# A hand-written order for the first feed-forward stage, with its first-batch products in the rounds that end attention

## The chip, the cores and the metric

One core of a Trainium2 chip. The metric is the device time of one execution in microseconds; a time is the median of several executions. Engines: PE (TensorE, matrix products), PEld (its weight loads), DVE (VectorE), ACT (ScalarE), POOL (GpSimd), SP (the queue that issues the DMAs).

## The reference

Three stages on two batches (B = 2) of 448 tokens, 12 heads of 64:

```python
scores = scale * np.matmul(q, k.transpose(0, 1, 3, 2))      # causal mask, then softmax
attn_out = np.matmul(attn, v)                               # to x: (B, S, 768)

x_prev = x shifted by one token
xk = mu_k * x + (1.0 - mu_k) * x_prev
xr = mu_r * x + (1.0 - mu_r) * x_prev
k = np.maximum(xk @ w_k, 0.0)                               # 768 -> 1024
v = k * k @ w_v                                             # 1024 -> 768
r = 1.0 / (1.0 + np.exp(-(xr @ w_r)))                       # 768 -> 768
x2 = r * v

h = np.maximum(x2 @ w_in, 0.0)                              # 768 -> 1024
gate = sigmoid(conv over 3 tokens of h)
out = (h * gate) @ w_out                                    # 1024 -> 768
```

The weights come as 64-bit floats.

## The kernel before, in words

Every large product is made of three matmuls (mm3, L63): each operand is split in a high half, rounded to the fast format, and a low half, what the rounding left; high by high, high by low and low by high are summed in PSUM. The high half of a tile is made by split_h (L68), the low half by split_l (L76), a subtraction on DVE or POOL. On the profile's lines the three matmuls of every product are L64, L65 and L66, the high halves L70 (POOL) and L74 (ACT), the low halves L78.

Attention runs as a pipeline of 12 jobs, one for a batch and a pair of heads. One round of the pipeline touches five jobs at once (n, c, l, p, a: from the next job to the one three rounds ago). What each engine does in a round, and in which order, is a written list, ORDER (L426). In it kqT transposes q and k, sc makes the scores, red the row minima (DVE), exp the exponentials (ACT), norm the division (POOL), T the transposes of the probabilities (L290), C the copies of them out of PSUM (ACT, or DVE for banks 3 and 4), V the products with v (L307), out the copy to xT (ACT), and mixP, mixD, mixH, mixL the token mix xr of one job for the next stage, with mixP, mixH and mixL on POOL and mixD on DVE. The loop of rounds, i from -1 to 14, stands in a manual schedule, so this order is kept on PE, ACT, DVE and POOL. In the rounds 12 to 14 there is no next and no current job, and their entries are left out. In the first rounds small matmuls on the identity (keep_warm, L443) stand behind some entries.

The first feed-forward stage has weight columns wr0 to wr5 (128 columns of w_r each), then wk0 to wk7 (w_k), wv0 to wv5 (w_v), and the second wi0 to wi7 (w_in) and rows wo0 to wo7 (w_out). Each is loaded as raw 64-bit words (load, L111, tag "wraw", two buffers, issued by SP) and converted (convert, L126) in seven steps: Abs on ACT (L100), four integer steps on DVE (L102, L104, L106, L108), the high half on ACT (L74) and the low half on DVE (L78). The converted pair goes to one of three buffers (tag "whl"). A call of step does one of the seven, convert_next all that are left. In rounds 4 to 11 of attention the entries w call step; two weight columns are ready by the end of the loop, and a third and most of a fourth follow right behind (L466).

For each column the stage makes products with xr (768 inputs in six chunks) for both batches (token_mm, L359), pr0 to pr5; ACT copies them to sr, and mix makes one chunk of xk for both batches: scaling on ACT (L339), the sum on DVE (L343), the high half on ACT, the low half on POOL (L78). The products with w_k (pk), w_v (pv) and w_in (ph) follow in the same way. Outside the manual schedule a scheduler sets the order of the engines by its own estimate of the time: it may move a stage's instructions up between those of attention.

Of the kernel before, what the change touches and what calls it, by code (L numbers as in the profile page):

```python
# [13 lines left out]
AF = mybir.ActivationFunctionType  # L14
# [5 lines left out]
def kernel(  # L20
# [105 lines left out]
    def convert(raw, n, name, he, le, rows=False, own=()):  # L126
# [23 lines left out]
        fill=-1e9 / SCALE, base=0, pattern=[[-1, CP]], channel_multiplier=1,  # L150
# [37 lines left out]
    def big(tag, name):  # L188
        return (act if tag in early else act2).tile([P, 2, NT], F32R, tag=tag, name=name)
# [6 lines left out]
    xr = [big(f"Y{c}", f"xr{c}") for c in range(NC)]  # L196
# [10 lines left out]
    class Job:  # L207
# [59 lines left out]
        def exp(self, c, j):  # L267
            w, i = (c + 1) * CP, 2 * c + j
            self.p[j, c] = p = sp.tile([CP, w], F32, tag=f"p{c}{j}", name=f"p_{self.n}_{i}", bufs=2)
            nc.scalar.activation(  # L270
                p, self.s[c, j][:, :w], AF.Exp, bias=self.st[:, 0, i:i + 1], scale=-1.0,
                accum_out=self.st[:, 1, i:i + 1],
            )
# [51 lines left out]
            mix_l(1, xr[self.hp], self.b, self.hp)  # L325

        def w(self, _):
            if 4 <= self.i < 11:
                step()

    ms = {}

    def mix_p(kind, b, c):
        ms[kind, b, c] = m = mixp.tile([P, S], F32, tag="m", name=f"m{kind}_{b}_{c}")
        prev, a = xT[c][:, b, 0:S], kind * NC + c
        if kind:
            nc.gpsimd.tensor_scalar(m, prev, mu[:, 2 * NC + a:2 * NC + a + 1], 1.0, ALU.mult, ALU.mult)  # L337
        else:
            nc.scalar.activation(m, prev, AF.Copy, scale=mu[:, 2 * NC + a:2 * NC + a + 1])  # L339

    def mix_d(kind, b, c):
        m, a = ms[kind, b, c], kind * NC + c
        nc.vector.scalar_tensor_tensor(m, xT[c][:, b, 1:S + 1], mu[:, a:a + 1], m, ALU.mult, ALU.add)  # L343

    def mix_h(kind, dst, b, c):
        split_h("p" if kind else "s", dst[:, 0, TOK[b]], ms[kind, b, c])

    def mix_l(kind, dst, b, c):
        split_l("p", dst[:, 1, TOK[b]], ms[kind, b, c], dst[:, 0, TOK[b]])

    def mix(kind, dst, b, c):
        mix_p(kind, b, c)
        mix_d(kind, b, c)
        mix_h(kind, dst, b, c)
        mix_l(kind, dst, b, c)

    TOK = [slice(b * S, (b + 1) * S) for b in range(B)]

    def token_mm(name, w, x, late):  # L359

        n = len(x)
        out_ = [bank(f"{name}_{b}") for b in range(B)]
        for c, b in sorted(((c, b) for b in range(B) for c in range(n)), key=lambda k: (late and k[0] == n - 1, k[1])):
            t = TOK[b]
            wt, o = w[0], slice(c * P, c * P + P)
            mm3(out_[b], wt[:, 0, o], wt[:, 1, o], x[c][:, 0, t], x[c][:, 1, t], c == 0, c == n - 1)
        return out_

    ring = ["mm"]

    def bank(name):
        tag = ring[0]
        ring.append(ring.pop(0))
        return ps.tile([P, 512], F32, tag=tag, name=name, bufs={"sc": 4, "tr": TR, "po": PO}[tag])[:, :S]
# [32 lines left out]
    def step():  # L407

        if not running:
            running.append(steps_next())  # L410
        if next(running[0], running) is running:
            running.clear()

    def convert_next():
        step()
        while running:
            step()

    def take():

        while loaded and not loaded[0][0] and len(ready) <= AHEAD:
            convert_next()
        return ready.pop(0)
# [9 lines left out]
    ROUNDS_AGO = {"n": -1, "c": 0, "l": 1, "p": 2, "a": 3}  # L433
    order = [x.split(".") for x in ORDER.split()]
    jobs = []
    small_steps = small()
# [6 lines left out]
    def keep_warm(n):  # L443
        for _ in range(n):
            nc.tensor.matmul(warm[:, :P], ident, ident, start=True, stop=True)

    keep_warm(7)
    ET = mybir.EngineType
    with tc.manual_schedule(engines={ET.PE, ET.Activation, ET.DVE, ET.Pool}):
        for i in range(-1, B * NPAIR + 3):  # L450
            if 2 <= i + 2 < B * NPAIR:
                jobs.append(Job((i + 2) // NPAIR, (i + 2) % NPAIR))
                jobs[-1].load()
            if i in (0, 1, 2):
                next(small_steps, None)
            if i == 2:
                load_next()
            for who, what, *a in order:
                x = i - ROUNDS_AGO[who]
                if 0 <= x < B * NPAIR and (i >= 0 or who == "n"):  # L460
                    getattr(jobs[x], "T_" if what == "T" else what)(*(int(y) if y.isdigit() else y for y in a))

                    if i < 1 and what in ("kqT", "sc", "T"):
                        keep_warm(3)

    convert_next()  # L466
    for _ in range(5):
        step()
    actx.close()
    ring[:] = ["sc", "sc", "tr", "sc", "sc", "tr", "tr", "po"]  # L470
    act2 = ctx.enter_context(tc.tile_pool(name="act2", bufs=1, reuse_waits="tile"))
    xk = [big(f"X{c}", f"xk{c}") for c in range(NC)]
    sr = [act2.tile([P, NT], F32, tag=f"U{e}", name=f"sr{e}") for e in range(NE)]
    for e in range(NE):
        w = take()
        for b, pr in enumerate(token_mm(f"pr{e}", w, xr, e == 0)):
            nc.scalar.activation(sr[e][:, TOK[b]], pr, AF.Copy)
        for b in range(B):
            mix(0, xk[e], b, e)
    pinned[0] = False  # L480
    wo_t = act.tile([P, 7, 2, WT], F32R, tag="T", name="wo_t")
    wo_slots += [wo_t[:, i] for i in range(7)]
# [2 lines left out]
    for f in range(NF):  # L485
        w = take()
        k2.append(big(f"Y{f}", f"k2_{f}"))
        for b, pk in enumerate(token_mm(f"pk{f}", w, xk, f == 0)):
            t = TOK[b]
            a = mixp.tile([P, S], F32, tag="m", name=f"a{f}_{b}")  # L490
# [8 lines left out]
    for e in range(NE):  # L499
        w = take()  # L500
        x2.append(big(f"X{e}", f"x2_{e}"))
        tc.keep_in_program_order(nc.scalar.activation(sr[e], sr[e], AF.Sigmoid))
        for b, pv in enumerate(token_mm(f"pv{e}", w, k2, e == 0)):
            t = TOK[b]
            a = mixp.tile([P, S], F32, tag="m", name=f"xv{e}_{b}")
# [9 lines left out]
    for f in range(NF):  # L515
        w = take()
# [29 lines left out]
    for o0 in range(0, len(outs), 6):  # L546
# [46 lines left out]
```

## Time and profile before

| | us |
|---|---|
| median of 3 executions | 406.72 (406.42 to 408.78) |
| the profiled execution | 408.7 |
| its span in the trace | 406.9 |
| PE busy | 390.5 (96%) |
| DVE busy | 307.4 (76%) |
| ACT busy | 233.8 (57%) |
| POOL busy | 126.1 (31%) |

Attention takes the time to about 119, the products with w_r to 165, those with w_k to 225, w_v to 285, w_in to 344, w_out to the end. In the timelines a row gives the start and the length of one instruction or of several like ones, and in brackets how long the engine stood idle before it and what ended that. A 128x448 matmul is shown with its passage through the array (0.36); the next may start 0.207 later. A DVE or ACT row, too, may begin some 0.08 before the one ahead of it ends. A busy share is of the engine's own time; an engine that stands idle off the path costs nothing. The granted clock (PEclk) is the share of 2.4 GHz that TensorE got, so 0.50 is the level of 1.2 GHz.

### The profile page before, as it was taken

The page shows a single profiled execution, that of the slowest core. Times are in us where ns is not written, and L with a number is a line of the kernel's source. Part 1 is how long each engine was busy: PE and PEld are TensorE (multiplying, and loading weights), DVE is VectorE, ACT ScalarE, POOL GpSimd, SP SyncE. Part 2 cuts the span into 40 slices and gives each one's busy share as a digit, 9 for nine tenths or more (in the row PEclk, how much of TensorE's full clock was granted, in tenths as well). Part 3 has the DMA queues.
Part 4 walks back from the last instruction along what each step waited for, and adds up shares of the span by engine and source line. Part 5 has one row for each costly group of instructions (what it writes and reads, how often), then busy time and mean ns, then how long its engine had stood idle before and what let it go on. Part 6 is the DMA issues. An engine that isn't in the chain of part 4 may idle for free.

```text
span 406.9 us, 6520 instructions
## 1 busy us (share of the span) xinstructions
PE 390.5 (96%) x2308; PEld 339.5 (83%) x2308; DVE 307.4 (76%) x610; ACT 233.8 (57%) x510; POOL 126.1 (31%) x177
## 2 busy tenths in 40 slices
PE   7999999999976699999999999999999999999996
PEld 7877677677744489999999999999999999999995
DVE  1689999999129997888987999888799999940000
ACT  2598999997237563486767943635344564423110
POOL 1158899999435541000000000000025142420000
PEclk9999999999996979999999999999999999999999
DMA  7446643512002225634463562442422220003111
GB/s 167 108 93 168 169 103 85 145 26 79 0 2 77 77 78 165 192 109 157 154 204 110 178 208 77 156 155 77 156 79 77 79 77 2 1 2 135 39 59 40
DMA packets 60157, 41.35 MB, mean 102 GB/s; under 512 B 34232, under 2 KB 59100, under 8 KB 60124
## 3 DMA queue, kind: packets, MB, share of 16 engines
q1 hardware_dynamic: 60124, 40.93, 33.5%
q8 instruction: 18, 0.29, 0.3%
q14 instruction: 15, 0.12, 0.1%
HBM read 38.17 MB, written 2.75 MB: 101 GB/s over the span
## 4 chain that ended last, share of the span: by engine, by line
PE 93%; DVE 5%; issue 1%; ACT 0%; POOL 0%; ACTq 0%; POOLq 0%
PE sc L251 7%; PE pp L290 6%; PE po L307 6%; PE ph L64 5%; PE pv L65 5%; PE pv L64 5%; PE pk L65 5%; PE pk L64 5%; PE ph L66 5%; PE ph L65 5%; PE pv L66 5%; PE pk L66 5%; PE pout L65 5%; PE pout L66 5%; PE pout L64 5%; PE pr L64 3%
## 5 line engine op out<-in xcount | busy, mean ns | idle before, releaser
L531 POOL TENSOR_TENSOR cv<-cv,hT 128x448 f32<-128x448 f32 x16 | 22.8, 1423 | 183.2 <-ACT cv L530 183.2
L282 POOL TENSOR_SCALAR p<-p,st 112x112 f32<-112x112 f32 (+1 forms) x96 | 52.4, 564 | 22.0 <-DVE st L278 19.4
L270 ACT ACTIVATE p<-s,st 112x112 f32<-112x112 f32 (+3 forms) x96 | 50.5, 534 | 2.0 <-DVE st L262 2.0
L262 DVE CUSTOM_DVE_ANT_0 s<-sc,maskw 112x112 f32<-112x112 f32 (+3 forms) x96 | 39.3, 438 | 5.3 <-PE sc L251 3.9
L251 PE MATMUL sc<-kT,qT 64*112 64x112 f32 (+3 forms) x288 | 30.7, 324 | 0.4 <-DVE kT L78 0.4
L290 PE MATMUL pp<-ident,p 112*112 112x112 f32 x240 | 28.3, 264 | 0.0
L290 PEld LDWEIGHTS pp<-ident,p 112*112 112x112 f32 x240 | 23.1, 133 | 6.2 <-issue 3.1
L343 DVE SCALAR_TENSOR_TENSOR m<-xT,mu,m 128x448 f32<-128x448 f32 x24 | 20.5, 862 | 8.1 <-POOL m L337 8.1
L558 ACT ACTIVATE osb<-pout 128x384 f32<-128x384 f32 x14 | 6.9, 492 | 34.3 <-PE pout L66 34.2
L307 PE MATMUL po<-pt,rv 112*64 112x448 f32 (+3 forms) x192 | 25.7, 407 | 0.0
L251 PEld LDWEIGHTS sc<-kT,qT 64*112 64x112 f32 x288 | 19.2, 172 | 6.5 <-DVE kT L78 0.5
L298 ACT COPY pt<-pp 112x448 f32<-112x448 f32 x36 | 19.2, 535 | 7.7 <-PE pp L290 7.6
L307 PEld LDWEIGHTS po<-pt,rv 112*64 112x64 f32 x192 | 12.5, 136 | 11.7 <-issue 4.7
L78 POOL TENSOR_TENSOR xk<-m,xk 128x448 fp32r<-128x448 f32 x12 | 17.2, 1440 | 14.8 <-ACT xk L74 14.8
L298 DVE COPY pt<-pp 112x448 f32<-112x448 f32 x24 | 13.5, 605 | 8.7 <-PE pp L290 8.7
L530 ACT ACTIVATE cv<-cv 128x448 f32<-128x448 f32 x16 | 9.3, 580 | 17.9 <-DVE cv L527 17.9
L270 ACT ACTIVATION_READ_ACCUMULATOR p<-s,st 112x1 f32 x96 | 19.4, 202 | 0.0
L78 POOL TENSOR_TENSOR xr<-m,xr 128x448 fp32r<-128x448 f32 x12 | 16.3, 1358 | 1.0
L65 PE MATMUL pout<-wo_t,g 128*128 128x384 f32 x49 | 16.5, 336 | 0.0
L66 PE MATMUL pout<-wo_t,g 128*128 128x384 f32 x49 | 16.5, 336 | 0.0
L64 PE MATMUL pout<-wo_t,g 128*128 128x384 f32 x49 | 16.4, 335 | 0.0
L74 ACT ACTIVATE g<-cv 128x448 fp32r<-128x448 f32 x16 | 9.2, 576 | 10.3 <-POOL cv L531 10.2
(501 smaller groups left out, 1231.3 us busy)
## 6 DMA issues: line engine op xcount, KB each, us to landing
rq<-in_q_dram SPq DMA_DIRECT2D x24, 112.0 KB, 2.6
rk<-in_k_dram SPq DMA_DIRECT2D x24, 112.0 KB, 2.6
rv<-in_v_dram SPq DMA_DIRECT2D x24, 112.0 KB, 2.5
out_dram<-osb SPq DMA_DIRECT2D x14, 192.0 KB, 1.9
wv0raw<-in_moe_w_v_dram SPq DMA_DIRECT2D x1, 1024.0 KB
wv1raw<-in_moe_w_v_dram SPq DMA_DIRECT2D x1, 1024.0 KB, 6.7
wv2raw<-in_moe_w_v_dram SPq DMA_DIRECT2D x1, 1024.0 KB, 5.0
wv3raw<-in_moe_w_v_dram SPq DMA_DIRECT2D x1, 1024.0 KB, 4.9
```

Source lines behind the costliest of these rows:

```text
L64: nc.tensor.matmul(ps_out, lh, rh, start=first, stop=False)
L65: nc.tensor.matmul(ps_out, lh, rl, start=False, stop=False)
L66: nc.tensor.matmul(ps_out, ll, rh, start=False, stop=last)
L78: e.tensor_tensor(out_, x, f32(h), ALU.subtract)
L251: nc.tensor.matmul(scs[j][:CP, :w], qT[r, 1 if pi == 2 else 0, c * CP:(c + 1) * CP], kT[r, 1 if pi == 1 else 0, :w], start=pi == 0, stop=p ...
L262: nc.vector.tensor_tensor_reduce(s_sb[:, :w], self.scs[c][j][:CP, :w], maskw[:, S - w:], -SCALE, 3e38, ALU.add, ALU.min, self.st[:, 0, i:i ...
L270: nc.scalar.activation(p, self.s[c, j][:, :w], AF.Exp, bias=self.st[:, 0, i:i + 1], scale=-1.0, accum_out=self.st[:, 1, i:i + 1],)
L282: nc.gpsimd.tensor_scalar(self.p[j, c], self.p[j, c], self.st[:, 2, i:i + 1], 1.0, ALU.mult, ALU.mult)
L290: nc.tensor.transpose(pp[:CP, i * CP:(i + 1) * CP], self.p[j, c][:, kc * CP:(kc + 1) * CP], ident[:CP, :CP])
L298: (nc.vector.tensor_copy if bi in TURN_V else nc.scalar.copy)(pt, self.pp[bi][:CP, :S])
L307: nc.tensor.matmul(self.po[j * D:(j + 1) * D, c0 * CP:S], self.raw["v"][:, kc, j], pt[:, off:off + S - c0 * CP], start=kc == 0, stop=self. ...
L531: nc.gpsimd.tensor_tensor(a, a, hc, ALU.mult)
```

## The change

The products of the first three weight columns with batch 0 (pr0_0, pr1_0, pr2_0: 18 matmuls each) are written into the rounds 12 and 13, in the places of entries whose jobs don't exist (INSTEAD, a table of how many chunks go where). The conversion steps there go on in round 11 and 12 in the places of other absent entries (STEPS), and one entry w more is used. The manual schedule now holds until the end of the products with w_r: each column's conversion, the two mixes, the copies to sr and the products are in written order. The mixes are done batch by batch (all six chunks of batch 0, then of batch 1) instead of chunk by chunk. Their low half goes from POOL to DVE. The ring of PSUM banks begins with the four score banks. Some warm-up matmuls go or move.

```diff
         def w(self, _):
-            if 4 <= self.i < 11:
+            if 4 <= self.i < 12:
                 step()
...
     def mix_l(kind, dst, b, c):
-        split_l("p", dst[:, 1, TOK[b]], ms[kind, b, c], dst[:, 0, TOK[b]])
+        split_l("p" if kind else "v", dst[:, 1, TOK[b]], ms[kind, b, c], dst[:, 0, TOK[b]])
...
-    ring = ["mm"]
+    ring = ["sc"] * 4 + ["tr"] * 3 + ["po"]
...
+    FIRST = 3
+    def fill():
+        for e in range(FIRST):
+            wrs.append(ready.pop(0))
+            prs[e, 0] = bank(f"pr{e}_0")
+            for c in range(NC):
+                products(prs[e, 0], wrs[e], xr, 0, NC, c)
+                yield
+    filler = fill()
+    INSTEAD = {"kqT.q": 1, "kqT.k": 1, "sc.0": 1, "sc.1": 1, "sc.2": 2, "sc.3": 2,
+               "T.0": 1, "T.1": 1, "T.2": 1, "T.3": 1, "T.4": 1}
+    STEPS = {11: ("kqL.q", "kqL.k"), 12: [f"red.{c}.{j}" for c in range(NQ) for j in range(2)]}
...
-                    if i < 1 and what in ("kqT", "sc", "T"):
-                        keep_warm(3)
-
-    convert_next()
-    for _ in range(5):
-        step()
+                if i == 0 and what in ("kqT", "sc") or i < 0 and op in ("kqT.k", "sc.3"):
+                    keep_warm(3 if op != "kqT.k" else 6)
+            elif x >= NJ:
+                if NJ <= i < NJ + 2:
+                    for _ in range(INSTEAD.get(op, 0)):
+                        next(filler, None)
+                if op in STEPS.get(i, ()):
+                    step()
+    for _ in filler:
+        pass
...
-    for e in range(NE):
-        w = take()
-        for b, pr in enumerate(token_mm(f"pr{e}", w, xr, e == 0)):
-            nc.scalar.activation(sr[e][:, TOK[b]], pr, AF.Copy)
-        for b in range(B):
-            mix(0, xk[e], b, e)
+    todo = [(b, c) for b in range(B) for c in range(NC)]
+    def mix_next():
+        b, c = todo.pop(0)
+        mix(0, xk[c], b, c)
+    for e in range(FIRST):
+        keep_sr(e, 0)
+    for e in range(FIRST):
+        prs[e, 1] = bank(f"pr{e}_1")
+        for c in range(NC):
+            products(prs[e, 1], wrs[e], xr, 1, NC, c)
+        if e:
+            convert_next()
+        mix_next()
+        keep_sr(e, 1)
+        if not e:
+            convert_next()
+        mix_next()
+    for e in range(FIRST, NE):
+        w = ready.pop(0)
+        for b in range(B):
+            prs[e, b] = bank(f"pr{e}_{b}")
+            for c in range(NC):
+                products(prs[e, b], w, xr, b, NC, c)
+        convert_next()
+        mix_next()
+        for b in range(B):
+            keep_sr(e, b)
+        mix_next()
+    manual.close()
```

On PE, where round 11 ends (pp_1_4_4 and the like are the transposed probabilities of job 10, by bank; pr0_0 is column 0 of batch 0), the order before is:

```order
L290 MATMUL pp_1_4_4_1902<-ident_70,p_1_4_5_1778 112x112
L290 MATMUL pp_1_4_4_1902<-ident_70,p_1_4_7_1722 112x112
L64 MATMUL pr0_0_2050<-xr0_84,wr0hl_1305 128x448
L65 MATMUL pr0_0_2050<-xr0_84,wr0hl_1305 128x448
L66 MATMUL pr0_0_2050<-xr0_84,wr0hl_1305 128x448
L64 MATMUL pr0_0_2050<-xr1_85,wr0hl_1305 128x448
```

and with the change:

```order
L290 MATMUL pp_1_4_4_1907<-ident_70,p_1_4_5_1778 112x112
L290 MATMUL pp_1_4_4_1907<-ident_70,p_1_4_7_1722 112x112
L290 MATMUL pp_1_4_0_1922<-ident_70,p_1_4_0_1692 112x112
L290 MATMUL pp_1_4_0_1922<-ident_70,p_1_4_2_1739 112x112
L290 MATMUL pp_1_4_0_1922<-ident_70,p_1_4_4_1811 112x112
L290 MATMUL pp_1_4_0_1922<-ident_70,p_1_4_6_1711 112x112
L290 MATMUL pp_1_4_2_1930<-ident_70,p_1_4_2_1739 112x112
L290 MATMUL pp_1_4_2_1930<-ident_70,p_1_4_4_1811 112x112
L290 MATMUL pp_1_4_2_1930<-ident_70,p_1_4_6_1711 112x112 x2
L64 MATMUL pr0_0_1940<-xr0_84,wr0hl_1305 128x448
```

The transposes of banks 0 and 2 have moved ahead of the first product, which stood behind bank 4.

On DVE, in the stage with w_r (m0_1_4 is the mix of batch 1, chunk 4, for xk; wr5c and wr5hl a weight under conversion and its halves), the order before is:

```order
L108 SCALAR_TENSOR_TENSOR wr4c_2155<-wr4raw_2022,wr4c_2155 128x768
L102 TENSOR_SCALAR wr5c_2216<-wr5c_2216 128x768
L343 SCALAR_TENSOR_TENSOR m0_1_4_2331<-xT_82,mu_80,m0_1_4_2331 128x448
L104 TENSOR_SCALAR wr5c_2216<-wr5c_2216 128x768
L343 SCALAR_TENSOR_TENSOR m0_0_5_2387<-xT_82,mu_80,m0_0_5_2387 128x448
L106 SCALAR_TENSOR_TENSOR wr5c_2216<-wr5raw_2153,wr5c_2216 128x768
L78 TENSOR_TENSOR wr4hl_2161<-wr4c_2155,wr4hl_2161 128x768
L108 SCALAR_TENSOR_TENSOR wr5c_2216<-wr5raw_2153,wr5c_2216 128x768
L343 SCALAR_TENSOR_TENSOR m0_1_5_2392<-xT_82,mu_80,m0_1_5_2392 128x448
```

and with the change:

```order
L102 TENSOR_SCALAR wr5c_2204<-wr5c_2204 128x768
L104 TENSOR_SCALAR wr5c_2204<-wr5c_2204 128x768
L106 SCALAR_TENSOR_TENSOR wr5c_2204<-wr5raw_2161,wr5c_2204 128x768
L108 SCALAR_TENSOR_TENSOR wr5c_2204<-wr5raw_2161,wr5c_2204 128x768
L78 TENSOR_TENSOR wr5hl_2210<-wr5c_2204,wr5hl_2210 128x768
L343 SCALAR_TENSOR_TENSOR m0_0_4_2213<-xT_82,mu_80,m0_0_4_2213 128x448
L78 TENSOR_TENSOR xk4_2098<-m0_0_4_2213,xk4_2098 128x448
L343 SCALAR_TENSOR_TENSOR m0_0_5_2219<-xT_82,mu_80,m0_0_5_2219 128x448
L78 TENSOR_TENSOR xk5_2099<-m0_0_5_2219,xk5_2099 128x448
L102 TENSOR_SCALAR wk0c_2264<-wk0c_2264 128x768
```

Conversion steps of two columns and the mixes' sums stood mixed with one another; now one column's steps stand together, then two mixes, each with its low half, which POOL made before.

## Rows read from the trace of the kernel before

**Rows 1.** Busy time by engine, 97.5 to 151.0; the clock before DMA share and GB/s.
```profile
97.50:151.00 53.50, 43.11 (x208) 34.32 (x207) 36.64 (x43) 27.05 (x50) 28.39 (x29) 0.87 0.13 44
```

**Rows 2.** Waits of PE: for whom, us in total, times, longest.
```profile
PE pr L64 <- ACT wr2hl L74: 3.6, 1, 3.6
PE pr L66 <- DVE wr3hl L78: 3.2, 1, 3.2
PE pr L64 <- POOL xr L70: 2.0, 1, 2.0
```

**Rows 3.** Timeline of PE: first product, and the matmuls behind the waits.
```profile
97.50 0.45 PE L64 MATMUL pr<-xr,wr0hl 128*128 128x448 f32 x1
...
127.13 0.74 PE L64 MATMUL pr<-xr,wr2hl 128*128 128x448 f32 x1 [3.65 <-ACT wr2hl L74]
...
130.62 0.36 PE L64 MATMUL pr<-xr,wr2hl 128*128 128x448 f32 x1
...
141.52 0.74 PE L66 MATMUL pr<-xr,wr3hl 128*128 128x448 f32 x1 [3.16 <-DVE wr3hl L78]
...
147.82 0.37 PE L64 MATMUL pr<-xr,wr3hl 128*128 128x448 f32 x1
```

**Rows 4.** pk's first high-by-high matmuls, by tile: duration in ns, first and last start.
```profile
L64 PE MATMUL pk<-xk,wk0hl x12: 368/368/368, 165.8 to 172.6; 128*128 128x448 f32 x12
```

**Rows 5.** Timeline of PE at the start of the kernel.
```profile
5.67 1.51 PE L445 MATMUL warm<-ident 128*128 128x128 f32 x6
6.97 0.86 PE L231 MATMUL ptrk<-ident,rk 112*128 112x112 f32 x4
7.67 0.85 PE L445 MATMUL warm<-ident 128*128 128x128 f32 x6
...
10.33 0.87 PE L251 MATMUL sc<-kT,qT 64*112 64x448 f32 x6
```

**Rows 6.** Timeline of DVE: copy, mix, and conversion steps beside POOL and alone.
```profile
98.88 1.13 DVE L298 COPY pt<-pp 112x448 f32<-112x448 f32 x2
...
119.38 0.68 DVE L343 SCALAR_TENSOR_TENSOR m<-xT,mu,m 128x448 f32<-128x448 f32 x1 [8.05 <-POOL m L337]
...
128.91 1.49 DVE L102 TENSOR_SCALAR wr3c<-wr3c 128x768 f32<-128x768 f32 x1
...
166.71 0.55 DVE L102 TENSOR_SCALAR wk3c<-wk3c 128x768 f32<-128x768 f32 x1
...
168.88 0.96 DVE L108 SCALAR_TENSOR_TENSOR wk3c<-wk3raw,wk3c 128x768 int32<-128x768 int32 x1
169.76 0.95 DVE L78 TENSOR_TENSOR wk2hl<-wk2c,wk2hl 128x768 fp32r<-128x768 f32 x1
...
179.67 0.62 DVE L78 TENSOR_TENSOR k<-a,k 128x448 fp32r<-128x448 f32 x1
```

**Rows 7.** ACT, 119 to 175: groups by line with mean ns, then three of its timeline.
```profile
L339 ACT ACTIVATE m<-xT,mu 128x448 f32<-128x448 f32 x12 | 7.8, 661 | 0.0
L74 ACT ACTIVATE xk<-m 128x448 fp32r<-128x448 f32 x12 | 6.9, 577 | 4.9 <-DVE m L343 4.8
L477 ACT ACTIVATE sr<-pr 128x448 f32<-128x448 f32 x12 | 6.2, 533 | 0.3 <-PE pr L66 0.3
...
130.32 0.91 ACT L100 ACTIVATE wr4c<-wr4raw 128x768 f32<-128x768 f32 x1 [0.94 <-DMA wr4raw<-in_moe_w_r_dram]
...
141.50 0.92 ACT L100 ACTIVATE wr5c<-wr5raw 128x768 f32<-128x768 f32 x1 [2.09 <-DVE wr3hl L78]
...
163.09 0.84 ACT L74 ACTIVATE wk1hl<-wk1c 128x768 fp32r<-128x768 f32 x1
```

**Rows 8.** Busy time of PE and PEld, line 307 from 97.5, line 290 from 101.
```profile
97.50:121.00 23.50, 4.66 (x32) 1.94 (x32) 1.00 0.00 1
...
101.00:121.00 20.00, 3.39 (x28) 2.91 (x28) 1.00 0.00 1
```

**Rows 9.** Busy time by engine, wk4's first DVE step to wv0's last; columns as rows 1.
```profile
179.19:221.40 42.21, 42.21 (x207) 38.33 (x205) 35.91 (x53) 30.16 (x51) 0.00 (x0) 1.00 0.47 151
```

More of the change, by code (lines that the diff above doesn't have):

```diff
@@ L357, with products @@
     TOK = [slice(b * S, (b + 1) * S) for b in range(B)]
+    def products(out_, w, x, b, n, c):
+        t, o = TOK[b], slice(c * P, c * P + P)
+        mm3(out_, w[0][:, 0, o], w[0][:, 1, o], x[c][:, 0, t], x[c][:, 1, t], c == 0, c == n - 1)
     def token_mm(name, w, x, late):
@@ L363, in token_mm @@
         for c, b in sorted(((c, b) for b in range(B) for c in range(n)), key=lambda k: (late and k[0] == n - 1, k[1])):
-            t = TOK[b]
-            wt, o = w[0], slice(c * P, c * P + P)
-            mm3(out_[b], wt[:, 0, o], wt[:, 1, o], x[c][:, 0, t], x[c][:, 1, t], c == 0, c == n - 1)
+            products(out_[b], w, x, b, n, c)
         return out_
-    ring = ["mm"]
+    ring = ["sc"] * 4 + ["tr"] * 3 + ["po"]
     def bank(name):
@@ L447 @@
     keep_warm(7)
-    ET = mybir.EngineType
[L449 to L461, printed above, removed]
-                    if i < 1 and what in ("kqT", "sc", "T"):
-                        keep_warm(3)
@@ L466 @@
-    convert_next()
-    for _ in range(5):
-        step()
+    FIRST = 3
+    wrs, prs = [], {}
+    def fill():
[8 more added lines that the diff above has]
+               "T.0": 1, "T.1": 1, "T.2": 1, "T.3": 1, "T.4": 1}
@@ new lines @@
+    STEPS = {11: ("kqL.q", "kqL.k"), 12: [f"red.{c}.{j}" for c in range(NQ) for j in range(2)]}
+    NJ = B * NPAIR
+    ET = mybir.EngineType
+    manual = ctx.enter_context(ExitStack())
+    manual.enter_context(tc.manual_schedule(engines={ET.PE, ET.Activation, ET.DVE, ET.Pool}))
+    for i in range(-1, NJ + 3):
+        if 2 <= i + 2 < NJ:
+            jobs.append(Job((i + 2) // NPAIR, (i + 2) % NPAIR))
+            jobs[-1].load()
+        if i in (0, 1, 2):
+            next(small_steps, None)
+        if i == 2:
+            load_next()
+        for who, what, *a in order:
+            x = i - ROUNDS_AGO[who]
+            op = ".".join([what] + a)
+            if 0 <= x < NJ and (i >= 0 or who == "n"):
+                getattr(jobs[x], "T_" if what == "T" else what)(*(int(y) if y.isdigit() else y for y in a))
+                if i == 0 and what in ("kqT", "sc") or i < 0 and op in ("kqT.k", "sc.3"):
[6 more added lines that the diff above has]
+                    step()
@@ L469 @@
+    for _ in filler:
+        pass
     actx.close()
-    ring[:] = ["sc", "sc", "tr", "sc", "sc", "tr", "tr", "po"]
     act2 = ctx.enter_context(tc.tile_pool(name="act2", bufs=1, reuse_waits="tile"))
@@ L473, with keep_sr @@
     sr = [act2.tile([P, NT], F32, tag=f"U{e}", name=f"sr{e}") for e in range(NE)]
-    for e in range(NE):
-        w = take()
-        for b, pr in enumerate(token_mm(f"pr{e}", w, xr, e == 0)):
-            nc.scalar.activation(sr[e][:, TOK[b]], pr, AF.Copy)
-        for b in range(B):
-            mix(0, xk[e], b, e)
+    def keep_sr(e, b):
+        nc.scalar.activation(sr[e][:, TOK[b]], prs[e, b], AF.Copy)
+    todo = [(b, c) for b in range(B) for c in range(NC)]
[17 more added lines that the diff above has]
+        w = ready.pop(0)
+        for b in range(B):
+            prs[e, b] = bank(f"pr{e}_{b}")
[7 more added lines that the diff above has]
+    manual.close()
     pinned[0] = False
```

## The prediction

> **What bounds the kernel now.** I read the busy time by stage first, then the waits of TensorE, its timeline around them, and then the DVE and ACT timelines that feed it. TensorE is the bound: outside one stretch it never stands still. In that stretch, from the first product of the feed-forward stage (97.50) to 151.0, it is busy for 43.1 of 53.5 us at a mean granted clock of 0.87 [rows 1]. So 10.4 us are idle. The waits [rows 2] name them: weight column wr2 came late from ACT (3.6), wr3 late from DVE (3.2), and 2.0 on POOL's xr, which is the end of attention itself. On top, matmuls behind the two long waits ran at the 1.2 GHz level: eight starts from 127.13 to 130.62 took 3.49 us and seventeen from 141.52 to 147.82 took 6.30 [rows 3]; at 0.207 each (in wk0's products 33 starts take 6.8 us, within their rounding [rows 4]) they would have taken 1.66 and 3.52, so 4.6 us went to the clock. In all 15.0 us could be won here. Everything after 165.8, where wk0 begins, is a full TensorE. The reader should also see that the rounds at the end of attention are not empty now: pr's first product already starts at 97.50 [rows 3]. What lacks is converted weights, not matmuls to put there.
>
> **Part by part.** I work by positions on the clock of the profiled execution (span 406.9, whole execution 408.7, which is 2.0 above the median of 406.72).
>
> *Start.* Of the groups of three warm-up matmuls ahead of job 0's scores, the one behind ptrq and the one behind sc.0 go, and the one behind ptrk has six. In before sc.3 starts at 10.33; the group behind ptrq takes 1.30 us ahead of ptrk and the next some 0.8 ahead of sc.0 [rows 5]. Afterwards: ptrk at 5.67 if rk is there, six warm matmuls (twelve in the trace, 1.30 + 0.8) from 6.4 to 8.5, sc.0, shorter than sc.3's 0.87, in 0.65, sc.3 at 9.15. That is 1.2 us early, and as TensorE is full from there to 97, it stays. Bounds: 0 if rk lands late, 1.9 if the warm matmuls all run at the 0.13 spacing. I take 1.2.
>
> *End of attention.* In round 11 no filler stands yet: TensorE goes from pp bank 4 straight to banks 0 and 2 of job 10, where 18 products stood. Bank 2 needs the DVE copy that stood at 98.88 [rows 6]. Ahead of it the change puts wr2's first step on ACT (0.91) and its second on DVE: 0.55 alone, 1.49 beside POOL [rows 6, 7]. With hops of about 0.4 the copy comes at 101.2 (100.6 to 102.2) and the first product at 102.2 (101.5 to 103.1), 4.7 later than now. From there TensorE has 216 products at 0.207 (44.8), the P·V matmuls 4.7 and 20 of 28 transposes of 3.4, so 2.4 [rows 8]: 51.9, with nothing to wait for (wr2 is done near 107.5; the last xr, by before's chain from attention's last matmul over ACT, POOL, DVE and POOL, comes some 3 us before it is wanted). wk0 can begin at 154.1 instead of 165.8 [rows 4]: **minus 11.7**. POOL loses 12 low halves, beside which a DVE step takes 1.49 for 0.55; DVE gets 12 of 0.62 for them [rows 6], 7.4 in all, which the cycle below contains.
>
> *The new supply of weights.* This decides. The order of ACT and DVE is now written out, and it is serial: a conversion, then a mix, then a mix, each a ping-pong. From the rows, one cycle counted from the start of Abs on ACT: Abs 0.91; the four DVE steps 3.13 (166.71 to 169.84); ACT high half 0.84; DVE low half 0.95, so low ready at +5.9 and high at +4.9; then per mix DVE 0.68, ACT 0.58, DVE 0.62, with ACT's scaling (0.66) and one copy of sr (0.53) in front of the second [rows 6, 7]. Overlapping the issue by 0.08, the next Abs stands at +9.3, at +9.8 where two copies lie between. TensorE takes a weight in 7.45. Three weights are ready ahead; the fourth needs the buffer of wr0, free after 72 products: 102.2 + 14.9 + 7.1 = 124.2. Copy, wr3, one mix: Abs of wr4 at 127.4. So wr5 136.7, wk0 146.1, wk1 155.9, wk2 165.6. Wanted: wr4 and wr5 are early; wk0 low half 152.0, wanted 154.5, early by 2.5. wk1 high half 160.8, wanted 159.1: 1.7, and 0.2 on its low half. wk2 is interleaved with wk3 on DVE, high 171.3, low 173.2; TensorE has done all the products that don't need it by 168.4: 2.9 + 1.1. wk3: wants the buffer of wk0, whose last products wait for the last mix (180.9), so 0.7 + 0.2. Sum **plus 6.8**.
>
> *Behind it.* DVE then runs full. From wk3's low half (184.0) to wv0's its operations add to 35.5 without waits; in before the same stretch had 35.9 busy in 42.2 [rows 9], so waits lie between 0 and 6.3. With 4, wv0 comes at 223.4 and TensorE, there at 220.5 and in need of it 0.9 later, loses **2.0** (0 to 4). In the later stages DVE has idle time again, so nothing more.
>
> *Clock.* The wait of 2.0 at 121.0 left the spacing at 0.207; the ones of 3.6 and 3.2 were followed by the 1.2 GHz level [rows 2, 3]. wk2's pair (2.9, 1.1) is like the latter: 2.9 of price by that row, of which the late last mix hides part; at attention's end the waits are shorter. I take **1.0**, bounds 0 and 4.6. The Trainium skill (TensorE: Matmul & The Clock Gate, What's actually happening) says the clock follows how busy the array has been lately and halves when it idles; by that rule the sparse stretch at 98 to 102 could cost too, and with 2.9 there the time would be 406.5. The trace agrees for the two long waits and shows no fall after the 2.0.
>
> Sum: -1.2 - 11.7 + 6.8 + 2.0 + 1.0 = -3.1. 408.7 - 3.1 = 405.6 for an execution like the profiled one, 403.6 beside the median.
>
> **Rivals.** *Supply keeps up (faster).* If a cycle takes no more than 7.45, wk1 to wk3 are never late and the clock holds: 403.6 - 7.8 = 395.8. For it: DVE's own work in a cycle is only 6.2 (3.1 + 0.9 + two of 1.1), and POOL no longer slows it [rows 6]. Against it: the order allows no overlap of the two ping-pongs, and the hops are in the rows. Chance 0.27, with all that is faster than 401.
>
> *The serial order is slower still.* The one whole cycle that before shows with two mixes in it, wr4's Abs to wr5's, took 11.2 (130.32 to 141.50) [rows 7]. If the new order needs that, wk2's Abs comes 4 x 11.2 after 127.4, at 172.2, 6.6 later, and as everything behind follows it the time is 410.2, 411 with the clock of a longer wait. It decides from 10.2 a cycle (gain gone) and costs 1% from 11.2. Against it: those 11.2 hold steps stretched beside POOL, like the 1.49 for 0.55 [rows 6]. Chance 0.13.
>
> *It doesn't do what it says.* Before already has pr's products in those rounds [rows 3]; if the first product waits till 103.1 (+0.9), the start brings nothing (+1.2) and wv0 waits 1.0 longer, the supply of weights alone sets the end and the time is 406.7. Chance 0.10.
>
> **How the numbers follow.** The forecast, a gain that is mostly given back through wk1, wk2 and wv0, has 0.50: 403.6. A change below about 1% (4.07 us) can't be told from none here. Low end: start 1.9 (-0.7), first product at 101.5 (-0.7), no wait at wv0 (-2.0), clock 0 (-1.0), cycles without the copies at 8.9 (-1.9): 397.3. High end: start 0, first product 103.1 (+0.9), half the clock's upper bound more (+1.8), two more at wv0 (+2.0): 409.5. With the outer cases partly in: 397.5 to 410. Faster by over 1% is below 402.65: the fast rival, 0.27, and 0.15 of the forecast's 0.50. Slower: 0.13. The rest, 0.45, is the same.
>
> **What would show it.** Right: TensorE starts pr near 101 to 102 and then runs without a wait over 0.5 us to wk0 (153 on the new start); waits on ACT and DVE for wk1 and wk2 of 1.5 to 4 us; Abs of wr4, wr5, wk0, wk1 9 to 10 us apart; no low half on POOL after the last xr, and L102 at 0.55 throughout. sc.3 at about 9.2. Wrong: a cycle of 8 or of 11; a wait before wk0; a low clock around 102; a wait in the wk stage above 4 us that isn't wk2; or a DVE that stays behind into the third stage.

## The result, and the profile after

The changed kernel takes 402.85 us (median of 4 executions, 401.71 to 403.38), the kernel before beside it 406.91 (4, 406.42 to 408.78): ratio 0.9888, interval 0.985 to 0.9926, a gain of about 1%. Twelve more executions (the first experiment) gave 404.44 against 407.22, ratio 0.9933, interval 0.99 to 0.9965. By these two medians the gain is 0.7 to 1.1%. The forecast of 403.6 lies between the two medians.

The profiled execution of the changed kernel is its lowest (401.71, span 399.9), that of the kernel before lies high (408.7). The two traces are 7.0 us apart, so that some 3 us of what they differ by is no gain of the change; where those come from is told last.

First the waits of TensorE (columns as in [rows 2]), without one at the start that both kernels have:

```profile
PE pk L64 <- ACT wk1hl L74: 3.2, 1, 3.2
PE pp L290 <- DVE pt L298: 1.9, 2, 1.1
...
PE pk L64 <- ACT wk2hl L74: 1.7, 1, 1.7
PE pk L64 <- ACT wk3hl L74: 1.5, 1, 1.5
PE pp L290 <- ACT pt L298: 1.4, 1, 1.4
PE pv L66 <- DVE wv0hl L78: 0.9, 1, 0.9
PE pk L66 <- DVE wk2hl L78: 0.7, 1, 0.7
PE pv L64 <- ACT wv0hl L74: 0.4, 1, 0.4
```

The waits on wr2, wr3 and xr [rows 2] are gone. In their place stand the same kind of wait one stage later (wk1 to wk3, 7.1 us in all), 1.3 us for wv0, and 3.3 us on pt, the copies of transposed rows at attention's end, which the kernel before did not have: 1.4 and 1.1 ahead of the first product with w_r, and 0.8 at 109.1, behind it.

The busy time by stage, columns as in [rows 1]; the first row runs from the first product of the feed-forward stage to wk0, the second is the stretch of [rows 1] itself, the last answers to [rows 9]:

```profile
98.94:150.72 51.78, 50.74 (x271) 44.46 (x270) 31.99 (x45) 20.85 (x36) 13.15 (x15) 1.00 0.21 67
97.50:151.00 53.50, 51.39 (x274) 45.08 (x275) 33.40 (x50) 22.57 (x40) 13.91 (x16) 1.00 0.21 67
150.72:220.00 69.28, 61.81 (x291) 54.96 (x290) 58.01 (x85) 50.58 (x89) 0.00 (x0) 0.98 0.42 133
...
183.00:222.00 39.00, 37.69 (x183) 34.03 (x183) 36.44 (x54) 33.04 (x58) 0.00 (x0) 1.00 0.50 162
```

Where [rows 1] had 43.11 us of TensorE at 0.87 of the clock there are now 51.39 at 1.00. The hole has not closed, it has moved: from 150.72 to 220 TensorE is idle for 7.5 us, in a stretch that was full before.

TensorE's timeline at the places of [rows 3, 4]: the first product, the start of wk0, the three late weights of that stage, and wv0:

```profile
98.94 0.45 PE L64 MATMUL pr<-xr,wr0hl 128*128 128x448 f32 x1
...
150.72 0.37 PE L64 MATMUL pk<-xk,wk0hl 128*128 128x448 f32 x1
...
158.92 0.74 PE L64 MATMUL pk<-xk,wk1hl 128*128 128x448 f32 x1 [3.17 <-ACT wk1hl L74]
159.46 0.58 PE L65 MATMUL pk<-xk,wk1hl 128*128 128x448 f32 x1
...
161.70 0.42 PE L66 MATMUL pk<-xk,wk1hl 128*128 128x448 f32 x1
...
169.47 0.47 PE L64 MATMUL pk<-xk,wk2hl 128*128 128x448 f32 x1 [1.67 <-ACT wk2hl L74]
...
182.11 0.47 PE L64 MATMUL pk<-xk,wk3hl 128*128 128x448 f32 x1 [1.54 <-ACT wk3hl L74]
...
219.53 0.47 PE L64 MATMUL pv<-k,wv0hl 128*128 128x448 f32 x1 [0.38 <-ACT wv0hl L74]
```

Behind the 3.17 seven distances take 2.78 us (158.92 to 161.70), the 1.2 GHz level, where 0.203 each would be 1.42: the clock cost 1.4 us there.

The supply: the first step (Abs) of five conversions on ScalarE, and the high half of one of them.

```profile
125.12 0.90 ACT L100 ACTIVATE wr4c<-wr4raw 128x768 f32<-128x768 f32 x1
...
134.56 0.89 ACT L100 ACTIVATE wr5c<-wr5raw 128x768 f32<-128x768 f32 x1
138.72 0.84 ACT L74 ACTIVATE wr5hl<-wr5c 128x768 fp32r<-128x768 f32 x1 [3.27 <-DVE wr5c L108]
...
144.00 0.90 ACT L100 ACTIVATE wk0c<-wk0raw 128x768 f32<-128x768 f32 x1
...
153.86 0.90 ACT L100 ACTIVATE wk1c<-wk1raw 128x768 f32<-128x768 f32 x1
...
163.73 0.89 ACT L100 ACTIVATE wk2c<-wk2raw 128x768 f32<-128x768 f32 x1
```

They stand 9.44, 9.44, 9.86 and 9.87 us apart, against the 7.3 that TensorE takes for a weight (36 products at 0.2027). VectorE in the same cycle:

```profile
135.49 0.56 DVE L102 TENSOR_SCALAR wr5c<-wr5c 128x768 f32<-128x768 f32 x1 [0.17 <-ACT wr5c L100]
...
139.60 0.96 DVE L78 TENSOR_TENSOR wr5hl<-wr5c,wr5hl 128x768 fp32r<-128x768 f32 x1 [0.97 <-ACT wr5hl L74]
...
141.80 0.62 DVE L78 TENSOR_TENSOR xk<-m,xk 128x448 fp32r<-128x448 f32 x1 [0.64 <-ACT xk L74]
```

No step of these cycles is stretched any more (0.56, where [rows 6] had 1.49 beside GpSimd), and VectorE waits for ScalarE where ScalarE had just waited 3.27 us for it: neither is full, each waits for the other.

### The profile page after: what moved, and what is told of

Read it like the earlier page. It is cut to its first block, busy times and chain, and to the rows that moved or that the text cites. A ratio compares the mean times of both kernels' runs of the same rounds, so it can differ in the third digit from the quotient of the medians.

```text
span 399.9 us, 6521 instructions
## 1 busy us (share of the span) xinstructions
PE 382.3 (96%) x2308; PEld 335.7 (84%) x2308; DVE 304.6 (76%) x622; ACT 233.7 (58%) x510; POOL 110.2 (28%) x165
## 4 chain that ended last, share of the span: by engine, by line
PE 59%; DVE 24%; ACT 9%; issue 4%; DMA 3%; POOL 1%; ACTq 0%; DVEq 0%; SPq 0%; POOLq 0%
PE pv L66 5%; PE pout L65 5%; PE ph L66 5%; DVE s L262 5%; PE ph L64 5%; PE ph L65 5%; PE pout L66 5%; PE pout L64 5%; PE pv L64 5%; PE pv L65 5%; PE sc L251 3%; PE warm L447 3%; PE po L307 3%; DVE m L343 3%; PE pp L290 2%
## 5 line engine op out<-in xcount | busy, mean ns | idle before, releaser
L586 POOL TENSOR_TENSOR cv<-cv,hT 128x448 f32<-128x448 f32 x16 | 21.4, 1340 | 216.9 <-ACT cv L585 216.9
L282 POOL TENSOR_SCALAR p<-p,st 112x112 f32<-112x112 f32 (+1 forms) x96 | 56.2, 602 | 20.6 <-DVE st L278 19.8
L290 PEld LDWEIGHTS pp<-ident,p 112*112 112x112 f32 x240 | 23.1, 133 | 10.4 <-issue 3.0
L343 DVE SCALAR_TENSOR_TENSOR m<-xT,mu,m 128x448 f32<-128x448 f32 x24 | 17.4, 723 | 8.9 <-ACT m L339 6.0
L581 DVE SCALAR_TENSOR_TENSOR cv<-hT,cw,cv 128x448 f32<-128x448 f32 x16 | 14.8, 927 | 0.1
L65 PE MATMUL pout<-wo_u,g 128*128 128x384 f32 x42 | 14.1, 336 | 0.0
```

The source lines that it names most:

```text
L282: nc.gpsimd.tensor_scalar(self.p[j, c], self.p[j, c], self.st[:, 2, i:i + 1], 1.0, ALU.mult, ALU.mult)
L290: nc.tensor.transpose(pp[:CP, i * CP:(i + 1) * CP], self.p[j, c][:, kc * CP:(kc + 1) * CP], ident[:CP, :CP])
L586: nc.gpsimd.tensor_tensor(a, a, hc, ALU.mult)
```

## The experiments

Kernels measured together ran on one chip, beside the same executions of the kernel before. Between chips the ratio to that kernel is safer than a difference in microseconds. All edits are small; where a diff has no other note it is against the changed kernel.

**The changed kernel again**, unedited, in 12 executions.

> The changed kernel once more, in more executions. Its four ran from 401.7 to 403.4, and the kernel before from 404.3 to 408.9 in 29; in the traces so far the distance of two products of the later stages is either 0.2026 or 0.2067 us, and it changes only behind a wait of TensorE. Theory: which of the two follows a wait is not set by the kernel; then some executions of the changed kernel lie up to 4 us above the first four, the median at 403 to 405 and this trace may show 0.2067 behind a wait. Rival: the changed kernel keeps 0.2026 always, and half of its gain is that: then 402.5 to 403.3 again and 0.2026 throughout.

Measured: 404.44 (402.05 to 407.52). So the spread belongs to the kernel, as the theory had it; its trace, though, has 0.2067 only from 208 to 222 and 0.2027 in all later stages. Another source of spread shows better. Of the changed kernel's sixteen executions so far, the six at a mean granted clock of 0.996 took 401.7 to 402.6 us, and the ten at a lower one 403.1 to 407.5. One place where the clock falls is attention's end. Here is TensorE in this trace:

```profile
97.75 0.59 PE L290 MATMUL pp<-ident,p 112*112 112x112 f32 x4 [1.43 <-ACT pt L298]
99.44 0.99 PE L290 MATMUL pp<-ident,p 112*112 112x112 f32 x4 [1.09 <-DVE pt L298]
100.11 0.72 PE L64 MATMUL pr<-xr,wr0hl 128*128 128x448 f32 x1
100.63 0.57 PE L65 MATMUL pr<-xr,wr0hl 128*128 128x448 f32 x1
```

and the busy time from 98 to 106 (PE busy, granted clock, DMA share, GB/s), in this execution and then in the first profiled one:

```profile
98.00:106.00 8.00, 6.91 (x27) 0.57 0.22 66
```

```profile
98.00:106.00 8.00, 7.18 (x48) 1.00 0.30 97
```

The same two waits (1.43 and 1.09 here, 1.40 and 1.09 there) were followed by the 1.2 GHz level in one execution and not in the other. From the first product to wk0 it takes 53.20 us here (100.11 to 153.31) and 51.78 there. The old-start and the GpSimd kernel below have the same two waits, and the clock falls behind them too (0.66 from 98 to 108, and 0.79 from 98 to 106); in three others with these waits it stays at 1.00. That makes three traces of seven.

**The start alone, in the kernel before**, and **the old start in the changed kernel.**

```diff
-                    if i < 1 and what in ("kqT", "sc", "T"):
-                        keep_warm(3)
+                    if i == 0 and what in ("kqT", "sc") or i < 0 and op in ("kqT.k", "sc.3"):
+                        keep_warm(3 if op != "kqT.k" else 6)
```

> The kernel before with the new start alone: the extra products on the identity go behind the first job's four score steps and key transposes as in the changed kernel, nothing else differs. My sum had -1.2 us for it (405.7 beside the 406.9 of the kernel before); the changed kernel's trace runs some 2.3 us earlier from the first job on, which would give 404.6. Rival: the start is absorbed by a later wait of the attention rounds and gives nothing (406.9). A second rival makes the start the whole net gain of the change, so that the moved work pays nothing: 402.9 from this alone.

> The changed kernel with the start of the kernel before. If start and moved work add up, it is the changed kernel's 402.9 plus what the start is worth: 404.1 by my term of 1.2, 405.2 by the 2.3 us that the trace shows. Rival: the start is the whole gain, then 406.9; or it is absorbed later, then 402.9.

Measured: 405.88 for the first (ratio 0.9988, interval 0.9965 to 1.0011), 404.37 for the second (0.9956, 0.9929 to 0.9984), against 404.44 (0.9933) for the changed kernel in as many executions. By time the start can't be told from nothing. By the traces it is there: the last group of score products of attention starts at 94.9 to 95.8 in the three traces with the old start, mean 95.5, and at 93.5 to 94.6 in the eleven with the new one, mean 94.1. That is 1.4 us, near the term of 1.2, and the spread of the later stages covers it. The second rival, that the start is the whole gain, is out.

**Conversions and mixings in turn.** The same instructions, with the seven steps of a conversion (the expectation says five) and the four of each mixing alternating:

```diff
+    def convert_and_mix(copies):
+        (b0, c0), (b1, c1) = todo.pop(0), todo.pop(0)
+        step()
+        mix_p(0, b0, c0)
+        step()
+        mix_d(0, b0, c0)
+        step()
+        mix_h(0, xk[c0], b0, c0)
+        mix_p(0, b1, c1)
+        step()
+        mix_l(0, xk[c0], b0, c0)
+        mix_d(0, b1, c1)
...
-        convert_next()
-        mix_next()
-        for b in range(B):
-            keep_sr(e, b)
-        mix_next()
+        convert_and_mix([(e, b) for b in range(B)])
```

> The changed kernel; in the stage of the second batch's products the five steps of a conversion and the four of two mixings are issued in turn instead of one after the other, with the same instructions, so that neither ScalarE nor VectorE waits for the other's last result. My theory: the supply of weights is bound by that serial order (9.4 to 9.9 us a conversion, where TensorE needs 7.45). Interleaved, the sums of the instructions leave 6.7 to 6.9 us, the waits at wk1, wk2 and wk3 (3.2, 1.7, 0.7 and 1.5 us in the changed kernel) go, and with them the low clock behind the longest: 394 to 396. Rival: VectorE's throughput, or the arrival of the weights, sets the pace: then the distance of the first conversion steps stays above 9 us and the time at 402 to 404.

Measured: 393.43 (391.68 to 396.28), ratio 0.9685 to the kernel before, interval 0.9644 to 0.9725. Abs of wr4 to wk2 stands at 125.62, 132.06, 138.50, 145.38 and 152.26: a cycle of 6.4 to 6.9:

```profile
125.62 0.89 ACT L100 ACTIVATE wr4c<-wr4raw 128x768 f32<-128x768 f32 x1
132.06 0.89 ACT L100 ACTIVATE wr5c<-wr5raw 128x768 f32<-128x768 f32 x1
...
152.26 0.91 ACT L100 ACTIVATE wk2c<-wk2raw 128x768 f32<-128x768 f32 x1
```

What TensorE waits for in the whole kernel, above 0.3 us and behind the start:

```profile
PE pp L290 <- DVE pt L298: 1.9, 2, 1.1
...
PE pp L290 <- ACT pt L298: 1.4, 1, 1.4
PE pout L64 <- ACT hT L594: 0.8, 1, 0.8
```

All waits on weights are gone, wv0's with them. From 140 to 150 VectorE is busy for 9.09 us here and for 7.09 in the changed kernel, ScalarE for 5.83 and 4.49. The rival (VectorE's throughput or the arrival of weights) is out.

**The stage left to the scheduler.** The hand order ends ahead of the stage of the second batch's products:

```diff
+    manual.close()
     for e in range(FIRST):
         keep_sr(e, 0)
...
-    manual.close()
     pinned[0] = False
```

> The changed kernel with the hand order ended ahead of the stage of the second batch's products, so that the compiler's scheduler puts that stage in order, as it did before the change. It sends ScalarE's mixing steps ahead of the conversions' and the next conversion's first step ahead of the mixing of the last. Theory (the written order is serial and costs 7 us of waits): the cycle falls below 9 us, the waits at wk1 to wk3 shrink, and the time is 395 to 401. Rival: the scheduler puts the conversions later, TensorE then waits at wr4 or wr5 as in the kernel before, and the time is 404 to 408.

Measured: 392.41 (391.11 to 395.08), ratio 0.9662, interval 0.962 to 0.9704, below the expected range. The row of its busy time from 140 to 150 (TensorE, weight load, VectorE, ScalarE, GpSimd, as in [rows 1]):

```profile
140.00:150.00 10.00, 10.00 (x51) 9.27 (x50) 9.26 (x15) 6.16 (x9) 0.00 (x0) 1.00 0.51 157
```

So the written serial order of this one stage costs 10.4 us by the first median of the changed kernel and 12.0 by the second. With it undone, the change is worth 14.8 us. The cost lies in the order being serial, not in its being written by hand: the interleaved order is written by hand too, and its median is only 1.0 us above this one, with overlapping intervals.

**The low halves back on GpSimd.**

```diff
-        split_l("p" if kind else "v", dst[:, 1, TOK[b]], ms[kind, b, c], dst[:, 0, TOK[b]])
+        split_l("p", dst[:, 1, TOK[b]], ms[kind, b, c], dst[:, 0, TOK[b]])
```

> The changed kernel with the low halves of the second mixing back on GpSimd, as in the kernel before. By my account of the serial order it is the wait of VectorE for ScalarE's high half (0.97 us) and the low half (0.56 us) that leave VectorE's chain, twice a conversion, against VectorE's steps that are stretched beside GpSimd (0.55 to 1.49 us): the cycle goes from 9.4 to something between 7.5 and 9.5, and the time to 399 to 403. Rival: the move off GpSimd is what the change gains by; then the cycle is 10 or more and the time 405 to 407.

Measured: 406.83, ratio 1.0003, interval 0.9983 to 1.0023; 2.4 us above the changed kernel's 404.44. My expectation failed, for a plain reason: ScalarE does not wait for the low half. It goes from a high half straight to its next scaling, so VectorE's low half lay beside ScalarE's work and taking it away shortens nothing. What remains is the stretch: the first VectorE step of a conversion, after a low half on GpSimd that reaches into it (1.16 from 136.41):

```profile
137.15 0.83 DVE L102 TENSOR_SCALAR wr5c<-wr5c 128x768 f32<-128x768 f32 x1 [1.43 <-ACT wr5c L100]
```

0.83 for 0.56, and the cycle is 9.70 and 10.12 for 9.44 and 9.87: 1.0 us over four. What makes the other 1.4 of the 2.4 us stays open. The rival's cycle of 10 or more came with two copies only. Its time of 405 to 407 was met, but its claim needs the next run.

**The low halves on VectorE, in the kernel before**, the reverse of the edit above and nothing else.

> The kernel before with the low halves of the second mixing on VectorE, nothing else. There VectorE works without a pause from 121 to 166 us, and its steps beside GpSimd's low halves are stretched (0.55 to 1.49, 0.68 to 1.55, 0.95 to 1.90 us). Theory (the stretch delays wr2 and wr3): it gives up about as much in stretched steps as it takes on in 12 low halves of 0.62 us, and TensorE's waits of 3.6 and 3.2 us change by less than 1.5 us: 405 to 408. Rival (VectorE beside GpSimd is what the old stage suffers from): the waits shrink to half and the time to 402 to 404.

Measured: 399.48 (399.09 to 402.79), ratio 0.9831, interval 0.9799 to 0.9862: minus 7.0 us against 406.47, from one line, more than the whole change gives. Both of my ranges were too high. The busy time from 120 to 140, in the kernel before and then in this one (columns as in [rows 1]):

```profile
120.00:130.00 10.00, 4.58 (x13) 3.01 (x14) 9.97 (x11) 7.55 (x14) 6.02 (x6) 0.68 0.23 79
130.00:140.00 10.00, 7.52 (x35) 6.30 (x33) 9.97 (x12) 6.65 (x11) 4.88 (x4) 0.98 0.23 78
```

```profile
120.00:130.00 10.00, 6.42 (x16) 4.56 (x17) 10.00 (x15) 7.28 (x14) 1.51 (x2) 0.60 0.24 79
130.00:140.00 10.00, 9.02 (x39) 7.87 (x38) 9.79 (x16) 7.77 (x14) 0.00 (x0) 0.89 0.23 79
```

VectorE is full in both, but in the same 20 us it does 22 instructions there and 30 here, low halves included (one that lies across 130 stands in both rows). TensorE's waits for wr2 and wr3 shrink from 3.6 and 3.2 to 2.6 and 1.0. The first step of a conversion (L102) takes 0.55 to 0.56 in this stage, where [rows 6] had 1.49. The Trainium skill (SBUF — State Buffer, SBUF: two separate sides) calls the port pair that VectorE and GpSimd share an exclusive lock held for a whole instruction. The stretched steps of [rows 6] and their absence here agree with it. So the last run's rival was half right: the move off GpSimd is a large gain by itself, though in the changed kernel only 2.4 us of it show.

**The moved work alone**: the stage left to the scheduler and the low halves on GpSimd, both edits above together.

> The changed kernel with the stage of the second batch's products left to the scheduler and the low halves of the second mixing on GpSimd: of the change there remain the start, the moved products of the first batch and the moved conversions. So far, beside 406.9 of the kernel before: the start about -1, the low halves alone -7.0, everything but the hand order -14.5. If these add up, it takes 399 to 400.5 here. Rival: with three conversions already done in the last rounds of attention, VectorE has room in the stage and its stretched steps no longer hold TensorE; the low halves are then worth 3 us or less beside the moved work, and the time is 392.5 to 395.5.

Measured: 398.92 (396.51 to 399.48), ratio 0.9808, interval 0.9775 to 0.9841. The parts add up, to within 0.1 us of the expected range, and the rival is out: with the stage left to the scheduler the low halves are worth 6.5 us beside the moved work (398.92 to 392.41, on two chips) and 7.0 without it.

**Three products in round 11.** The wait for pt stands at the end of round 11, where the change puts no filler:

```diff
-                if NJ <= i < NJ + 2:
+                if NJ <= i < NJ + 2 or i == NJ - 1 and what == "sc":
```

> The changed kernel with three of the moved products also at the absent score steps of round 11, between the transposes, where TensorE waits 1.4 and 1.1 us for the copies of transposed rows. Theory: TensorE reaches wk0 1.5 to 2 us earlier, but ScalarE and VectorE are not earlier, so that the waits at wk1 to wk3 take it back: 402 to 403.5, as the changed kernel. Rival (TensorE's own path sets the end there): 400.5 to 401.5.

Measured: 401.18 (401.13 to 401.55), ratio 0.9871. The number is the rival's, and the theory's premise was wrong: the supply comes earlier too. Abs of wr4 starts at 124.29 for 125.12 and TensorE's first product of wk0 at 149.89 for 150.72, both 0.83 earlier, so nothing had to be given back:

```profile
PE pk L64 <- ACT wk1hl L74: 3.2, 1, 3.2
...
PE pp L290 <- DVE pt L298: 1.7, 2, 0.9
PE pk L64 <- ACT wk3hl L74: 1.4, 1, 1.4
```

The wait of 1.4 on ScalarE's pt is gone. The spread goes with it: five executions within 0.42 us, where the unedited kernel had 5.5. That fits the fall of the clock behind those waits: of the seven traces that have them three show it, of the four with round 11 filled none.

**Both, by hand and by the scheduler.** The interleaved order with the products in round 11, and the stage left to the scheduler with them:

> The interleaved conversions and mixings together with the three products in round 11. With the supply out of the way TensorE's path sets the end, so what round 11 saves should now stay: 391.5 to 392.5 where the interleaved kernel alone took 393.4. Rival (the copies that TensorE waits for come no earlier, and it waits as long for the transposes): 393 to 394.

> The changed kernel with the stage of the second batch's products left to the scheduler and three of the moved products in round 11. Round 11 was worth 2.9 us to the interleaved kernel (393.4 to 390.5) and should be worth as much here: 389.5 to 390.5 from 392.4, with no execution above 392. Rival: TensorE now reaches wk0 ahead of what the scheduler's order supplies and a wait of 1 to 3 us returns in the wk stage: 391 to 393.

Measured: 390.51 (389.29 to 391.01) for the first, ratio 0.9602, interval 0.9572 to 0.9633: 2.9 below the interleaved kernel, at a granted clock of 1.00 throughout. It has the lowest median of all the kernels here. The second missed its expectation: 393.33, two executions at 390.3 and four from 393.3 to 394.2, and no wait in its wk stage, which the rival had wanted. Its one new wait is this:

```profile
128.89 0.47 PE L66 MATMUL pr<-xr,wr3hl 128*128 128x448 f32 x1 [0.30 <-DVE wr3hl L78]
```

> The kernel of the run before last on round 11 once more, for its trace. Its executions lay at 390.3 (two) and 393.3 to 394.2 (four), and the traced one kept 0.2067 us between products from a 0.30 us wait at 128.9 to the end. Theory (the distance is settled anew at a wait, by chance): a trace near 390.3 shows 0.2026 behind the same wait, or no such wait; a trace near 393.5 shows 0.2067 again. Rival (the 3 us come from elsewhere, the weights or the start): the two times go with the same distance.

Measured: 393.98 (393.88 and 394.08), with the same wait and 0.2067 behind it. That agrees with the theory but does not show its other half, since neither execution lay at 390.3.

## Why the prediction was right, and where it was off

The story held: the moved products fill attention's end, TensorE runs through to wk0, and a serial order of ScalarE and VectorE takes most of it back in wk1 to wk3. By its steps:

- **Start, -1.2.** The traces show 1.4 on the mean at attention's end; the times can't separate it. That it came out near is in part luck: the first job's sc.3, due at 9.15, starts at 7.5 to 8.6 (9.5 to 10.4 with the old start), 2.0 us earlier on the mean, and 0.6 of that is lost on the way. "It stays" was wrong.
- **End of attention, -11.7.** From the first product to wk0 the forecast was 51.9, measured 51.78. So close is luck: the products follow each other at 0.2027 us there, not at 0.207 (0.9 less over 216), and a wait of 0.8 for pt at 109.1 stands where I had "nothing to wait for". The first product was due at 101.0 with the new start and came at 98.94 and 100.11 in the two traces, so wk0 stood at 150.72 and 153.31 where 153 was due. I had priced the wait for the copy of pp bank 2 as a position only. The runs showed that it is two waits, 1.4 and 1.1, that they can be had back (round 11's products: 1.7 to 3.3 us by the two medians, 2.9 in the interleaved kernel, nothing seen in the scheduler's), and that the clock falls behind them in some executions.
- **Supply, +6.8.** Measured 3.2 for wk1, 1.7 and 0.7 for wk2, 1.5 for wk3: 7.1. The forecast parts were 1.9, 4.0 and 0.9, so the sum is better than its parts: TensorE came to wk0 2.2 us ahead of the forecast and wk0's Abs only 0.9 (144.00, due at 144.9), which made wk1 later than forecast. The cycle was forecast at 9.3 and 9.8 and is 9.44 and 9.87. The step is shown as cause by the interleaved run, not only by the trace.
- **wv0, +2.0.** Measured 1.3. VectorE has 36.4 us of work in 39.0 there; I had put 4 us of waits, there are 2.6.
- **Clock, +1.0.** 1.4 behind wk1's wait alone, in the profiled execution. These 1.4 us probably only shortened the next wait, since wk2 was late by its own chain: in the second trace the clock held behind wk1's 3.15, and wk2's wait was 2.80, not 1.67. The forecast's 2.9 for such a fall is 2.8 by its own rows (6.30 less 3.52). Its reading that the clock did not fall after the 2.0 wait was too simple. In the kernel before, the granted clock is 1.00 from 121.0 to 123.4 and 0.54 on the mean from 123.4 to 127.1, so it fell within some 0.3 us of the start of the 3.65 wait, and what lay ahead of that wait, the 2.0 among it, had a part. In the moved-work kernel, too, a wait of 1.93 was followed 1.8 us later by the 1.2 GHz level. "A low clock around 102" was listed as what would make the prediction wrong; it appeared in one of the two traces of the changed kernel. The prediction weighed the rule of the Trainium skill (TensorE: Matmul & The Clock Gate, What's actually happening) at just this place and set it aside, and the runs say: sometimes. The rule's 406.5 lies within the executions measured, above their median.
- **In sum**: -3.1 forecast; -4.1 and -2.8 measured. Supply, wv0 and clock were forecast at 9.8 together and the waits and the clock of the profiled execution add to 9.8 (7.1, 1.3 and 1.4), though each term is off; errors that cancel have a share in the hit.

The rivals: a supply that keeps up would have given 395.8 by the prediction. The kernels where it keeps up take 393.4 and 392.4, 2.4 to 3.4 less. That sum had taken out the waits of the wk stage and the clock but kept 2.0 for wv0, whose wait goes too; the rest of the difference stays open. The slower serial order needed a cycle of 11.2; the largest seen is 10.12, with the low halves on GpSimd.

What the prediction did not price at all is the low halves by themselves. It counted 7.4 us on VectorE for them "which the cycle below contains", and set against that one stretched step. In the kernel before, where VectorE was full, they were the cheapest large gain: 7.0 us. In the changed kernel, where VectorE waits for ScalarE's answer, the same line is worth 2.4. The account by runs: moved work with the start -7.4, low halves -6.5, serial order of one stage +10.4 to +12.0, together -1.9 to -3.5, where -2.8 to -4.1 was measured directly; the parts come from several chips.

## What to carry to other kernels

Where two engines pass a tile to and fro, issue independent chains in turn, or let the scheduler do it: the sums of work on each engine (here 6.2 us on VectorE a cycle) say nothing about a cycle that is the length of the chain (9.4 to 9.9). When a change has several parts, price each alone, and try each alone: here a net gain of 1% was two gains of 7 us and a loss of 10 to 12. An engine that is always busy may still be slowed by a neighbour, as VectorE was beside GpSimd here; count its instructions per 10 us, not its busy share.

## What the runs showed that was not expected

*Two distances between products.* In the later stages products follow each other either at 0.2027 or at 0.2067 us, at a granted clock of 1.00 both times. The first product of wi0 and the first of the output stage, 288 products apart, in the interleaved kernel with round 11 filled:

```profile
266.49 0.36 PE L64 MATMUL ph<-x,wi0hl 128*128 128x448 f32 x1
...
324.86 0.34 PE L64 MATMUL pout<-wo_t,g 128*128 128x384 f32 x1
```

and in its sister with the stage left to the scheduler (first trace):

```profile
269.53 0.37 PE L64 MATMUL ph<-x,wi0hl 128*128 128x448 f32 x1
...
329.05 0.34 PE L64 MATMUL pout<-wo_t,g 128*128 128x384 f32 x1
```

58.37 us and 59.52. All fourteen traces show one of these two values in that stage, six the first and eight the second, the kernel before among the eight; four kernels run together on one chip show both. Within a trace the distance mostly changes behind a wait: in the moved-work kernel it is 0.2027 up to 220.28 and, past a stretch at the 1.2 GHz level, 0.2067 from 227.95 on, with this at the start of the change:

```profile
222.58 0.47 PE L64 MATMUL pv<-k,wv0hl 128*128 128x448 f32 x1 [1.93 <-ACT k L74]
```

But not only there. In the changed kernel with round 11 filled it goes from 0.2067 to 0.2027 at 204.3 with no wait at all, and in two traces (the changed kernel again, and the low halves on GpSimd) from 0.2027 to 0.2067 at 208 to 209, behind two steps of 0.23 to 0.31 us and no wait on record. So the expectation of the changed kernel's second run, that it changes only behind a wait, is too strong.

From wk0 to the output stage it makes 3.5 us (175.10 against 178.56 in the two kernels above), and 2.3 of the 7.0 us between the traces of before and after (4.7 at wv1, 7.0 at the end). The three kernels without any wait for a weight in the feed-forward stages kept 0.2027 from wk0 on. What picks the distance stays open: that it is chance was only argued, from a kernel whose executions lie at 390.3 and at 393.3 to 394.2.

*The same wait, two clocks.* 1.4 and 1.1 us of waiting with 0.6 us of work between were followed by the 1.2 GHz level in one execution and by the full clock in another of the same kernel (1.4 us of time up to wk0). The wait for wk1 shows the same the other way round: behind its 3.17 the first trace had the 1.2 GHz level, and the second, behind 3.15, the full clock for 2.8 us and more:

```profile
161.49 0.47 PE L64 MATMUL pk<-xk,wk1hl 128*128 128x448 f32 x1 [3.15 <-ACT wk1hl L74]
```

```profile
161.49:164.30 2.81, 2.81 (x13) 1.00 0.80 265
```

A wait can thus cost more than its length, and differently from one execution to the next. Why one execution falls and another doesn't, no run here shows.
